# Token rows' sums on GpSimd and a newly planned order in a recurrent attention kernel on one core

## The chip, the core and the metric

The kernel runs on one core of a Trainium2 chip. A core has a matrix engine (TensorE, PE in the profile, with its weight loads shown apart as PEld), VectorE (DVE), ScalarE (ACT), GpSimd (POOL) and SyncE (SP, which issues most DMAs). The engines run their own instruction streams in order and wait for each other by semaphores. The metric is device time of one launch in microseconds; lower is better.

## What is computed

A block of a language model: attention with a recurrent memory, then an MLP, both behind a layer norm and both added to the residual. The attention walks over 64 segments of 32 tokens, and each segment's 8 memory rows come from the segment before it. That is what makes the 64 steps sequential.

```python
x = A_x                                            # (1, 2048, 512)
h  = x + A(layernorm(x), mem0, Wq, Wk, Wv, Wo)     # 32 heads of 128
h2 = h + gelu(layernorm(h) @ w1 + b1) @ w2 + b2    # 512 -> 1792 -> 512

def A(x, mem, ...):
    for s in range(64):
        hs = concat([mem, x[32*s : 32*s + 32]])    # 8 memory rows + 32 tokens
        q, k, v = hs @ Wq, hs @ Wk, hs @ Wv
        p = softmax(where(mask, q @ k.T * scale, -1e9))
        o = (p @ v) @ Wo
        mem = o[:8]                                # into the next segment
        outs.append(o[8:])
```

The mask lets every row see the memory rows and makes the rest causal.

## The kernel before

**Tiling.** A segment's left operand is `hT`, 32 columns per chunk of 128 inputs: 24 token rows (`NA`) and the 8 memory rows. The matrix engine is used in four column groups of 32, so one "unit" of a projection is four matmuls of 128 x 32 weights (the tokens) against 512 columns of WQ, WK or WV. A half of a projection (`Q0`, `Q1`, `K0`, `K1`, `V0`, `V1`) has four units, one per chunk of the 512 inputs. The other 8 tokens of each segment are handled four segments at a time: block `bk` of 128 tokens has its 4 x 8 such rows in `hB`, and their projections and output projection are the filler parts `F0` and `F1`, run one block ahead (and one behind for the output, `wo_B`) in segments of blocks 1 to 14.

**One segment.** The parts are: projections; `SC0`, `SC1`, the scores of the memory and late rows, by `ZC` and `KALL`; their softmax on DVE and ACT (`nmc` row maximum, `Ea` and `EC` the exponentials of two halves, `ra`, `rsc` reciprocals, `PCa`, `PC` the normalised rows, `PTC` their transpose); `PV0`, `PV1` (times V), whose memory rows are copied to `OT` as `OTm0`, `OTm1`; `WO`, the output projection, in eight units; `SA`, the scores of the 24 token rows, whose softmax (`nma`, `SAs`, `SAe`, `sma`, `rsa`, `PA`, `PTA`, `BD`) feeds `PVA` in the *next* segment, copied to `OT` as `OTx`. So token rows run one segment behind for PV and two behind for WO, and only memory rows are in the recurrence.

**The end of a segment.** `wo` (L1179) leaves the projection in a PSUM bank as two halves, on partitions 0 to 63 and 64 to 127. DVE transposes it to `TT` (L1183) and adds the halves, by `halves_add` (L1176), twice each: for the memory rows into `hT` of the next segment (`hTm`, L1186), and for the token rows into `opT` (`opA`, L1195). When a block's `opT` is complete, `nat` transposes it by DMA and adds it to the residual.

**The order.** `ORDERS` (L37) gives the order of the units on the matrix engine, one list for each of s mod 4, written out by hand. All other operations are placed by a list scheduler that runs when the kernel is built (`schedule`, L236): each operation has an assumed duration; `PLAN` (L43) gives many of them a due time within the segment, by s mod 4; those without (`planned`, L108, returns None) are ranked by their distance to the end. Ready operations are taken by this key and put on their engine at the first gap that fits. Some may run on either of two or three engines; the scheduler picks the cheaper or the one named in `HOME` (L100). `BANK` (L42) gives each part its PSUM bank. `PHASE` (L25) fixes at which instruction of a segment the engine's blocks of 256 instructions begin, by adding weight loads. `directions` (L580) decides in which direction a part walks over the chunks so that loaded weights can be kept between parts. POOL's folds of the block rows (`fold`, L1232, called by `tail`, L1437) wait for PC of the second half and for the `opA` adds moved into the tail.

Of the kernel before, what the change touches and what calls it, by code (L numbers as in the profile page):

```python
# [24 lines left out]
PHASE = (0, 64, 128, 192)  # L25
# [11 lines left out]
ORDERS = ((('Q0', 0, 1), ('K0', 0, 1), ('Q0', 1, 2), ('K0', 1, 2), ('Q0', 2, 3), ('Q1', 0, 1), ('Q0', 3, 4), ('K0', 2, 4), ('Q1', 1, 4), ('K1', 0, 4), ('SC0', 0, 99), ('V0', 0, 1), ('V1', 0, 1), ('V0', 1, 4), ('F1', 0, 1), ('SC1', 0, 99), ('V1', 1, 2), ('F1', 1, 2), ('V1', 2, 4), ('F0', 0, 1), ('PV0', 0, 99), ('PVA', 0, 99), ('F1', 2, 3), ('WO', 0, 2), ('PV1', 0, 99), ('WO', 2, 8), ('F1', 3, 4), ('SA', 0, 99), ('F0', 1, 4)),  # L37
# [3 lines left out]
ORDER = ORDERS[0]  # L41
BANK = dict(K0=7, K1=6, Q0=6, Q1=5, V0=7, V1=5, F0=4, F1=6, FB=4, SA=5, WO=7, SC0=3, SC1=2)  # L42
PLAN = {"kq2": (1.72,) * 4,  # L43
        "QT0": (2.37,) * 4,
        "ZCm0": (2.85,) * 4,
        "kq0": (2.23,) * 4,
        "KA0": (2.87,) * 4,
        "SP0": (-1.81, -1.81, -1.52, -1.65),
        "nmc0": (3.86,) * 4,
        "Ea0": (4.18,) * 4,  # L50
        "EC0": (4.59,) * 4,
# [1638 lines left out]
```

## Time and profile before

| | us |
|---|---|
| median of 3 runs (807.34 to 808.39) | 807.91 |
| span of the profiled execution | 805.9 |
| PE / DVE / ACT / POOL busy | 775.0 / 621.0 / 527.1 / 349.6 |
| before the first segment's end, 0 to 51.64 | 51.64 |
| segments 1 to 63 (51.64 to 702.65) | 651.01 |
| MLP and the last outputs (702.65 to 805.90) | 103.25 |

The profile is one execution; its span is 2.0 us under the median of the runs. In a row of the timeline the columns are the start, the length, the engine, the line of the kernel, the operation, out<-in by the program's names and how many were merged. A row of the table of stretches has the length, and each engine's busy time and instructions, the granted clock and the DMA share.

### The profile page before, as it was taken

What the parts mean: (1) busy time and instruction counts of PE and PEld (TensorE: products, weight loads), DVE (VectorE), ACT (ScalarE), POOL (GpSimd) and SP (SyncE); (2) the same over time, 40 slices, a digit from 0 to 9 for tenths busy, and PEclk for the clock granted to TensorE, in tenths of its full rate; (3) what the DMA queues carried; (4) which work ended last, traced back from release to release, by engine and by line L of the source; (5) the groups of instructions that cost most, each with busy time, mean ns of one, the idle gap of its engine ahead of it and who ended that gap; (6) DMA issues with size and microseconds to landing.
All of it is one profiled execution on the core that took longest, in us unless ns stands there. A gap on an engine that the chain in (4) does not pass through costs nothing.

```text
span 805.9 us, 43594 instructions
## 1 busy us (share of the span) xinstructions
PE 775.0 (96%) x19308; PEld 422.5 (52%) x18891; DVE 621.0 (77%) x2008; ACT 527.1 (65%) x1522; POOL 349.6 (43%) x886
## 2 busy tenths in 40 slices
PE   3788999999999999999999999999999999999998
PEld 1345555555555555555555555555555555544443
DVE  3268897989898989898989898989899887824211
ACT  2446777777777777777777777777676766643342
POOL 5023334545454545454545454545463535267200
PEclk9989999999999999999999999999999999999999
DMA  9950010111101010101010202020212131264200
GB/s 340 392 185 16 4 29 11 30 31 29 31 21 39 17 43 17 43 11 50 9 45 10 50 11 50 11 49 3 51 29 62 40 86 29 88 170 130 69 27 26
DMA packets 65449, 48.03 MB, mean 60 GB/s; under 512 B 29028, under 2 KB 61676, under 8 KB 65260
## 3 DMA queue, kind: packets, MB, share of 16 engines
q1 hardware_dynamic: 64928, 44.98, 19.0%
q8 instruction: 150, 2.46, 1.2%
q14 instruction: 39, 0.32, 0.1%
q10 hardware_dynamic: 332, 0.27, 0.1%
HBM read 31.08 MB, written 8.13 MB: 49 GB/s over the span
## 4 chain that ended last, share of the span: by engine, by line
PE 91%; DVE 3%; DMA 2%; SPq 2%; ACT 1%; issue 1%; POOL 0%
PE ps L872 43%; PE ps L1171 16%; PE ps L605 6%; PE quad L1579 6%; PE ps L1572 5%; PE ps L1210 4%; PE quad L1075 3%; DMA WQ<-in_A_Wq_dram 2%; SPq L775 2%; PE ps L1105 2%; PE quad L1037 2%; PE ps L1365 2%; PE quad L1143 1%; PE quad L1080 1%; DVE PC L1062 1%; ACT kq L890 1%
## 5 line engine op out<-in xcount | busy, mean ns | idle before, releaser
L872 PE MATMUL ps<-WQ,hT 128*32 128x512 bf16 x2048 | 157.4, 382 | 3.4 <-DVE hT L1177 3.3
L1171 PE MATMUL ps<-WO,OT 128*32 128x256 bf16 x4224 | 140.8, 275 | 1.0 <-ACT OT L890 1.0
L872 PE MATMUL ps<-WV,hT 128*32 128x512 bf16 x1780 | 138.7, 379 | 0.0
L891 ACT ACTIVATE kq<-ps 128x512 bf16<-128x512 f32 x146 | 87.2, 597 | 63.7 <-PE ps L872 63.4
L1126 POOL TENSOR_TENSOR PA<-SA,rsa 128x256 bf16<-128x256 f32 x64 | 39.9, 624 | 183.0 <-DVE rsa L1119 170.6
L890 ACT CAST kq<-ps 128x512 bf16<-128x512 f32 x160 | 93.4, 584 | 38.2 <-PE ps L872 38.2
L1171 PEld LDWEIGHTS ps<-WO,OT 128*32 128x32 bf16 x4224 | 96.2, 97 | 26.5 <-ACT OT L890 12.3
L1132 POOL COPY BD<-PTA 32x192 bf16<-32x192 bf16 x256 | 95.5, 373 | 16.6 <-DVE PTA L1128 0.8
L1062 DVE SCALAR_TENSOR_TENSOR PC<-EC,rsc,even 128x128 bf16<-128x128 f32 x256 | 94.5, 370 | 6.7
L872 PE MATMUL ps<-WK,hT 128*32 128x512 bf16 x1292 | 92.5, 379 | 0.0
L872 PEld LDWEIGHTS ps<-WQ,hT 128*32 128x32 bf16 x2048 | 57.0, 96 | 57.9 <-issue 18.7
L913 DVE STREAM_TRANSPOSE KALL<-kq 128x256 f32<-128x256 f32 x160 | 70.5, 440 | 20.8 <-ACT kq L890 18.6
L1054 ACT ACTIVATE EC<-quad,nmc 128x64 f32<-128x64 f32 x252 | 77.1, 311 | 5.9 <-DVE nmc L1045 0.2
L605 PE MATMUL ps<-WK,hT 128*32 128x512 bf16 x756 | 74.6, 379 | 0.0
L890 ACT CAST VS<-ps 128x512 bf16<-128x512 f32 x126 | 73.7, 585 | 0.7
L890 ACT CAST OT<-quad 128x128 bf16<-128x128 f32 (+1 forms) x205 | 66.3, 363 | 7.5 <-PE quad L1080 5.7
L913 DVE STREAM_TRANSPOSE QT<-kq 128x256 f32<-128x256 f32 x128 | 57.0, 445 | 15.5 <-ACT kq L891 14.1
L872 PEld LDWEIGHTS ps<-WV,hT 128*32 128x32 bf16 x1780 | 50.5, 96 | 34.2 <-issue 1.0
L1575 ACT ACTIVATE WQ<-ps,b1t 128x512 bf16<-128x512 f32 x42 | 28.9, 688 | 52.0 <-PE ps L1572 52.0
L872 PEld LDWEIGHTS ps<-WK,hT 128*32 128x32 bf16 x1292 | 36.4, 97 | 46.1 <-issue 20.1
L1117 ACT ACTIVATE SA<-SA 128x256 f32<-128x256 f32 x64 | 26.7, 417 | 49.4 <-DVE SA L1116 45.0
L1223 POOL TENSOR_TENSOR opT<-TTB,TTS 32x64 bf16<-32x64 f32 x128 | 40.3, 315 | 31.7 <-DVE opT L1177 22.5
(160 smaller groups left out, 1477.9 us busy)
## 6 DMA issues: line engine op xcount, KB each, us to landing
WV<-in_A_Wv_dram SPq DMA_DIRECT2D x4, 1024.0 KB, 10.3
WK<-in_A_Wk_dram SPq DMA_DIRECT2D x4, 1024.0 KB, 18.0
WQ<-in_A_Wq_dram SPq DMA_DIRECT2D x4, 1024.0 KB, 19.0
WO<-in_A_Wo_dram SPq DMA_DIRECT2D x16, 256.0 KB, 7.6
v_last<-VSB SPq DMA_DIRECT2D x60, 64.0 KB, 3.1
VBD<-v_last SPq DMA_DIRECT2D x60, 64.0 KB, 2.8
h_mid<-xr SPq DMA_DIRECT2D x16, 128.0 KB, 1.8
WQ<-h_mid SPq DMA_DIRECT2D x4, 512.0 KB, 4.4
```

The lines of the kernel that those rows point to most:

```text
L605: return e.add_instruction(mybir.InstMatmult(name="I-%d" % (4000000 + _kept[0]), engine=mybir.EngineType.PE, start_tensor_calc=start, stop ...
L872: ins = e.matmul(o, l, m, start=(k == 0), stop=(k == DC - 1), tile_position=(0, 32 * j), skip_group_check=True)
L890: return {"act": (lambda e: e.copy(out, src), t_act(n, ps_)), "dve": (lambda e: e.tensor_copy(out, src), 0.155 + 1.0e-3 * n * fast)}
L891: return {"act": (lambda e: e.mul(out, src, scale_), t_act(n, ps_)), "dve": (lambda e: e.tensor_scalar(out, src, scale_, None, ALU.mult), ...
L913: S.op("dve", lambda e: e.transpose(out, src), reads=[("kq", i)], writes=[key], dur=t_dve(256) + 0.02)
L1054: return e.activation(EC[:, r, sl, :], o[:, sl, :], ACTF.Exp, bias=nmc[:, r, sl:sl + 1], accum_out=smc[:, r, sl:sl + 1])
L1062: S.op("dve", lambda e, sl=sl, xc=xc: e.scalar_tensor_tensor(PC[:, r, :, :, sl], xc, rsc[:, r, sl:sl + 1], ev, ALU.mult, ALU.mult), reads= ...
L1132: S.narrow(S.op("pool", lambda e, j=j, rows=rows: e.tensor_copy(BD[rows, par, :, j, :, :], PTA[rows, :, 0:NA, :]), reads=["PTA"], writes=[ ...
L1171: ins = e.matmul(ps[bank][32 * j:32 * j + 32, 0:256], lhs(slot(h)), wo_cols(h, b), start=(k == 0), stop=(k == 15), tile_position=(0, 32 * ...
L1223: return e.tensor_tensor(o[32 * q:32 * q + 32, c:c + 2], x, y, ALU.add)
L1572: ins = e.matmul(ps[bank][:, 0:SBT], W1[:, cc, fc * P:(fc + 1) * P], hnT_of(k)[:, cc, :], start=(cc == 0), stop=(cc == DC - 1))
L1579: S.op("pe", lambda e: e.matmul(quad[:, t, :], gT_of(k, fc)[:, t * P:(t + 1) * P], W2[:, fc, :], start=(fc == 0), stop=(fc == FC - 1)), re ...
```

## The change

- `wo`: the sum of the token rows' halves (`opA`) moves from DVE to POOL: one copy of partitions 0 to 63 of `TT` (token columns, `opS`) to partitions 64 to 127 of the scratch tile `TTS`, now 128 partitions high, then two adds, each on 64 partitions.
- `schedule`: operations without a due time get their rank scaled to the segments' pace and 2.1 us of lead; a planned operation may not be put ahead of one that was planned earlier on the same engine.
- `ORDERS`: K0 goes first in a segment, Q0 is done after six or seven units, SA goes behind the filler units in segments 0, 1 and 2 mod 4. `directions` is worked out for each of the four orders.
- `PLAN` and `HOME` are new throughout, each due time by s mod 4; `BANK` moves Q0 from bank 6 to bank 0; `PHASE` moves by 21 places.
- Eight banks become one PSUM tensor, `PC` and `PTC` become two tiles each, `b1n` lies in `oN`. The diff also has branches (`TT2`, `SPL`, `KCOL`, `PVM`, `NRM`, `P3`) whose switches are off.

```diff
-PHASE = (0, 64, 128, 192)
+PHASE = (235, 43, 107, 171)
+OPA = True
+AHEAD = 2.1
-ORDERS = ((('Q0', 0, 1), ('K0', 0, 1), ('Q0', 1, 2), ('K0', 1, 2), ('Q0', 2, 3), ('Q1', 0, 1), ('Q0', 3, 4), ('K0', 2, 4), ('Q1', 1, 4), ('K1', 0, 4), ('SC0', 0, 99), ('V0', 0, 1), ('V1', 0, 1), ('V0', 1, 4), ('F1', 0, 1), ('SC1', 0, 99), ('V1', 1, 2), ('F1', 1, 2), ('V1', 2, 4), ('F0', 0, 1), ('PV0', 0, 99), ('PVA', 0, 99), ('F1', 2, 3), ('WO', 0, 2), ('PV1', 0, 99), ('WO', 2, 8), ('F1', 3, 4), ('SA', 0, 99), ('F0', 1, 4)),
...
+ORDERS = ((('K0', 0, 1), ('Q0', 0, 2), ('K0', 1, 2), ('Q0', 2, 4), ('Q1', 0, 1), ('K0', 2, 4), ('Q1', 1, 4), ('K1', 0, 4), ('SC0', 0, 99), ('V0', 0, 4), ('V1', 0, 1), ('F1', 0, 1), ('SC1', 0, 99), ('V1', 1, 3), ('F1', 1, 2), ('F0', 0, 1), ('V1', 3, 4), ('PV0', 0, 99), ('PVA', 0, 99), ('F1', 2, 3), ('WO', 0, 2), ('PV1', 0, 99), ('WO', 2, 8), ('F1', 3, 4), ('F0', 1, 4), ('SA', 0, 99)),
...
-BANK = dict(K0=7, K1=6, Q0=6, Q1=5, V0=7, V1=5, F0=4, F1=6, FB=4, SA=5, WO=7, SC0=3, SC1=2)
+BANK = dict(K0=7, K1=6, KX=3, Q0=0, Q1=5, V0=7, V1=5, F0=4, F1=6, FB=4, SA=5, WO=7, SC0=3, SC1=2, SC2=1, PV0=7)
...
-        "VS1": (6.72,) * 4,
-        "OTm0": (6.56,) * 4,
-        "nma": (10.17,) * 4,
-        "PTA": (13.52,) * 4,
-        "BD": (15.41,) * 4,
-        "TT": (9.37,) * 4,
-        "hTm": (9.86,) * 4,
-        "opA": (17.5, 10.96, 18.73, 17.5),
+        "BD": (16.331, 0.007, 16.734, 15.95),
+        "OTm0": (5.545, 5.337, 3.85, -0.582),
+        "PTA": (13.188, 14.525, 13.433, 12.556),
+        "TT": (6.905, 7.221, 7.098, 0.097),
+        "VS1": (6.687, 6.87, 6.634, 6.858),
+        "hTm": (3.099, 7.229, 6.437, 5.811),
+        "nma": (-6.06, -1.636, 0.66, 3.743),
+        "opA0": (8.087, 8.613, 0.69, 8.76),
+        "opA1": (-1.074, 4.255, -1.419, -0.739),
+        "opS": (17.639, 3.506, 18.616, 20.489),
...
-HOME = {('SC0', 0): 'act', 'ZCm0': 'pool', 'kq1': 'act', 'SP1': 'act', 'VS1': 'act', 'OTm0': 'act', 'SAp': 'dve', 'PA': 'pool', 'VSB1': 'act'}
+HOME = {'SP1': 'act', 'SAp': 'dve', 'ZCm1': 'pool', 'ZCm0': 'pool', 'OTx0': 'dve', ('SA', 2): 'act', ('SC0', 0): 'dve', 'kq3': 'act', ('SC0', 3): 'dve', 'kq0': 'act', 'OTm1': 'act', ('SA', 1): 'act', 'kq4': 'act', ('SA', 0): 'act', ('SC1', 1): 'dve', 'VSB1': 'act'}
...
+        first, pace = base[1], 4 * STEP / (base[6] - base[10])
...
-                key = -o.rank - BONUS.get(o.kind, 0.0)
+                key = -(first - (first - o.rank) * pace) - AHEAD - BONUS.get(o.kind, 0.0)
...
-                i = bisect.bisect_right(ST, t)
+                i = max(bisect.bisect_right(ST, t), placed[eng] + 1 if fixed else 0)
...
+            if fixed:
+                placed[o.eng] = i
+            elif i <= placed[o.eng]:
+                placed[o.eng] += 1
...
-        TTS = sb("TTS", [64, 2, 4, 32], F32)
+        TTSX = sb("TTS", [P, 2, 4, 32], F32)
+        TTS = TTSX[0:64]
...
-                    o_ = S.op("dve", lambda e: [halves_add(tt, q2, o[64 * q2:64 * q2 + 64], slice(0, NA))(e) for q2 in range(2)][1],
-                         reads=[("TT", par)], writes=[("opA", (sx // 4) % 2, sx % 4)], dur=0.53, after=after)
+                    if OPA:
+                        v = TTSX[64:128].rearrange("p c q t -> p (c q t)")[:, 0:2 * DC * NA].rearrange("p (c q t) -> p c q t", c=DC, q=2)
+                        S.narrow(S.op("pool", lambda e: e.tensor_copy(v, tt[0:64, :, :, 0:NA]), reads=[("TTl", par)] * TT2 + [("TT", par)], writes=["opS"], dur=0.35, after=after))
+                        for q2 in range(2):
+                            S.narrow(S.op("pool", lambda e, q2=q2: e.tensor_tensor(o[64 * q2:64 * q2 + 64], tt[64:128, :, q2, 0:NA], v[:, :, q2], ALU.add),
+                                          reads=["opS", ("TT", par)] + [("TTl", par)] * TT2, writes=[("opA%d" % q2, (sx // 4) % 2, sx % 4)], dur=0.4, after=after))
+                        S.tag = was
+                        return
...
-                elif s % 4 in (3, 0) and 3 < s < NS - 2:
+                elif s % 4 in (3, 0) and 3 < s < NS - 2 and not OPA:
                     now.append(rows)
```

More of the change, by code (lines that the diff above doesn't have):

```diff
@@ L295, in schedule @@
         starts = {e: [] for e in ENGINES}
+        placed = {e: -1 for e in ENGINES}
         for o in order:
@@ L1027, in sc_mm @@
             reg = 2 + bk % 2
+            heads = range(4) if part is None else range(2 * part, 2 * part + 2)
             def f(e):
-                for i in range(4):
+                for i in heads:
                     for j in range(4):
@@ new lines, in normal, with pv_spread @@
+            S.op("dve", lambda e: e.transpose(PTC[r][:].rearrange("p k t a -> p (k t a)").bitcast(F32), PC[r][:].rearrange("p k t a -> p (k t a)").bitcast(F32)),
+                 reads=[("PCa", r)] * (not NRM >> r & 1) + [("PC", r)], writes=[("PTC", r)], dur=0.31)
+        def pv_spread(s):
+            for j in range(4):
+                rows = slice(32 * j, 32 * j + 32)
+                o, v = PB[rows, j].rearrange("p t a -> p (t a)"), PTC[0][rows, 0].rearrange("p t a -> p (t a)")
+                x = S.either({"act": (lambda e, o=o, v=v: e.copy(o, v), 0.26), "dve": (lambda e, o=o, v=v: e.tensor_copy(o, v), 0.2), "pool": (lambda e, o=o, v=v: e.tensor_copy(o, v), 0.3)},
+                             reads=[("PTC", 0)], writes=[("PB", j)])
+                x.thin = True
@@ L1081, in f @@
+                    ins = e.matmul(o, VBD[rows, bk % 2, sg, r, :], PTC[r][rows, :, 32:64, :].rearrange("p b q a -> p b a q"),
                                    start=False, stop=True, tile_position=(64 * t, 0), skip_group_check=True)
                 return ins
[L1083 to L1084 removed]
+            S.op("pe", f, reads=[("VS", s % 3, r), ("PTC", r)] + [("VBD", bk % 2, j) for j in range(4)], writes=both, dur=0.205, mode=MH, ni=20)
```

397 lines of the change are left out of this document (271 added, 126 removed), and 6 rows, old and new, of the table ORDERS.

## The prediction

> **What bounds the kernel now.** I read the page's busy shares first, then the busy time by stretches, each of four segments, that is one block of 128 tokens.
>
> ```profile
> span 805.9 us, 43594 instructions
> PE 775.0 (96%) x19308; PEld 422.5 (52%) x18891; DVE 621.0 (77%) x2008; ACT 527.1 (65%) x1522; POOL 349.6 (43%) x886
> core 0: us, PE busy (x) PEld busy (x) DVE busy (x) ACT busy (x) POOL busy (x), PEclk, DMA share, GB/s
> 244.77:285.92 41.15, 41.15 (x1172) 23.04 (x1125) 37.09 (x123) 30.07 (x91) 20.14 (x53) 1.00 0.12 29
> 285.92:327.07 41.15, 41.15 (x1172) 22.96 (x1125) 37.09 (x123) 30.07 (x91) 20.26 (x53) 1.00 0.11 29
> 615.54:657.34 41.80, 41.54 (x1173) 23.04 (x1125) 37.28 (x125) 30.28 (x91) 19.52 (x50) 1.00 0.19 51
> ```
>
> Four segments take 41.15 us again and again, 10.29 each, with PE covered from end to end. But PE rows overlap and their ends are modelled, so short waits hide in them. They come out by subtracting starts. The timeline of PE through one segment:
>
> ```profile
> 270.39 0.40 PE L605 MATMUL ps<-WK,hT 128*32 128x512 bf16 x4
> 270.61 0.83 PE L872 MATMUL ps<-WK,hT 128*32 128x512 bf16 x12
> ...
> 273.65 0.40 PE L872 MATMUL ps<-WV,hB 128*32 128x512 bf16 x4
> 274.00 0.26 PE L1075 MATMUL quad<-PTC,VS 64*128 64x32 bf16 x8
> 274.11 0.22 PE L1080 MATMUL quad<-PTC,VBD 64*128 64x128 bf16 x2
> ...
> 274.46 0.40 PE L872 MATMUL ps<-WV,hB 128*32 128x512 bf16 x4
> 274.75 0.62 PE L1171 MATMUL ps<-WO,OT 128*32 128x256 bf16 x16
> 275.31 0.26 PE L1075 MATMUL quad<-PTC,VS 64*128 64x32 bf16 x8
> 275.42 0.22 PE L1080 MATMUL quad<-PTC,VBD 64*128 64x128 bf16 x2
> 275.57 1.50 PE L1171 MATMUL ps<-WO,OT 128*32 128x256 bf16 x48
> 276.89 0.42 PE L1105 MATMUL ps<-KALL,QT 128*32 128x32 bf16 x32
> 277.14 1.06 PE L872 MATMUL ps<-WV,hB 128*32 128x512 bf16 x16
> 278.07 0.41 PE L872 MATMUL ps<-WQ,hT 128*32 128x512 bf16 x4
> ```
>
> A unit of four 512-wide matmuls costs 0.22 (270.39 to 270.61). Three places cost more. The unit at 273.65 takes 0.35 until PV0: 0.13 over. The unit at 274.46 takes 0.29 until WO: 0.07 over. The four units at 277.14 take 0.93 where 0.86 would do: 0.07 over. WO's 16 matmuls at 274.75 take 0.56 until PV1, where 16/48 of 1.32 (275.57 to 276.89) would be 0.44: 0.12 over. The 0.12 before PV1 is the nearest row for what a change of tile shape costs on PE, so of PV0's 0.13 only about 0.01 is a wait. The other two are waits, as the table of waits shows:
>
> ```profile
> PEld L870 <- DVE hT L1177: 24.8, 62, 1.3
> PEld ps L1171 <- ACT OT L890: 12.3, 62, 0.3
> PEld quad L1075 <- DVE rsc L1059: 31.6, 64, 0.9
> ```
>
> Each occurs in nearly every segment. The weight loads run ahead, so those sums are larger than what PE loses. So about 0.15 us of the 10.29 can be won by order, some 1.5%; the rest is matmuls and shape changes, which the diff leaves alone in number and kind.
>
> **What the change does, part by part.**
>
> *The wait before WO.* WO waits for OTm0, ACT's copy of PV0's memory rows. On ACT:
>
> ```profile
> 273.95 0.58 ACT L890 CAST VS<-ps 128x512 bf16<-128x512 f32 x1
> 274.42 0.29 ACT L890 CAST OT<-quad 128x128 bf16<-128x128 f32 x1
> ...
> 275.68 0.27 ACT L890 CAST OT<-quad 128x128 bf16<-128x128 f32 x1 [0.18 <-PE quad L1080]
> ```
>
> Here the second cast (PV1's copy) starts 0.26 after its last matmuls (275.42 to 275.68), on an ACT that was idle. The first starts 0.31 after (274.11 to 274.42): it stands behind the VS1 cast. In the new plan OTm0 has key 5.5, 5.3, 3.9, -0.6 and VS1 6.7, 6.9, 6.6, 6.9, and a planned operation may no longer be put ahead of an earlier planned one on its engine; so OTm0 goes first and VS1 follows. That saves 0.31 - 0.26 = 0.05. It is realised in full, since WO can move 0.07 before the unit ahead of it bounds it. VS1 then ends about 274.37 + 0.29 + 0.58 = 275.24, and PV1 starts at 275.31: just hidden. If that cover is gone, VS1's lateness takes back up to the 0.05. A unit stands between PVA and WO in blocks 1 to 14, 56 segments: 56 x 0.05 = **-2.8 us**.
>
> *The sums of token rows leave DVE.* Rows of what goes and of the nearest to what comes:
>
> ```profile
> L1177 DVE TENSOR_TENSOR opT<-TT 64x96 bf16<-64x96 f32 x128 | 33.8, 264 | 3.0
> L1225 POOL COPY TTS<-TTB 64x256 f32<-64x256 f32 x32 | 12.6, 393 | 36.2 <-DVE opT L1177 34.4 <-DVE TTB L1214 0.9
> L1226 POOL TENSOR_TENSOR TTB<-TTB,TTS 64x256 f32<-64x256 f32 x32 | 23.1, 722 | 14.2 <-DVE PC L1062 12.6
> L1223 POOL TENSOR_TENSOR opT<-TTB,TTS 32x64 bf16<-32x64 f32 x128 | 40.3, 315 | 31.7 <-DVE opT L1177 22.5
> ```
>
> Two adds per segment, 0.53 us, leave DVE, 33.8 us in all. POOL gets a copy of 192 columns (at most 0.39, as for 256) and two adds of 96 columns: 722 - 315 over 192 columns is 2.1 ns each, so 315 + 32 x 2.1 = 382 ns. Together 0.39 + 0.76 = 1.15 us a segment, 74 us in all. POOL has 41.15 - 20.14 = 21.0 us free in four segments, so 4.6 of it is covered. DVE's relief is worth nothing directly: the three DVE chains in PE's way run back to back from what ACT and PE release, and the opT adds were in none of them. What it does free is POOL's folding of TTB, which waited for those adds (the 34.4 and 22.5 above). How a fold collides with the adds of hTm, the last link before the next segment:
>
> ```profile
> 267.29 0.43 DVE L1177 TENSOR_TENSOR hT<-TT 64x32 bf16<-64x32 f32 x2
> 277.61 0.39 DVE L1177 TENSOR_TENSOR hT<-TT 64x32 bf16<-64x32 f32 x2
> 586.38 0.51 DVE L1177 TENSOR_TENSOR hT<-TT 64x32 bf16<-64x32 f32 x2
> 267.08 0.39 POOL L1225 COPY TTS<-TTB 64x256 f32<-64x256 f32 x1
> 586.32 1.14 POOL L1223 TENSOR_TENSOR opT<-TTB,TTS 32x64 bf16<-32x64 f32 x3
> ```
>
> 0.39 beside no such fold, 0.43 beside POOL's copy, 0.51 beside its adds. In segments 1 mod 4 (267.29) the fold came late because it waited for opT; now it can be earlier: -0.04 x 14 = -0.6. Against it the new copy may start right after the transpose to TT (key 3.5 in those segments), at the same place: +0.04 x 14 = +0.6. I take **0**, and 0.12 x 56 = 6.7 us as the upper bound, if every hTm meets an add; the lower bound is -0.6.
>
> The Trainium skill, "SBUF — State Buffer", section "Who interferes with whom", says that a VectorE instruction with two SBUF inputs and a GpSimd one that reads SBUF take one port pair as an exclusive lock, and that the second blocks until the first is done. By that rule a collision would cost hTm up to a whole POOL add, 0.37, and the bound would be 21 us. The rows show 0.12, so I keep that.
>
> *The order on PE.* K0 comes first, Q0 is complete after six or seven units in place of seven, K0 after eight or nine in place of nine; SC0 stays after 16, SC1 and PV0 behind the same count of units. SA moves behind the filler units F. Between WO's end and the next segment stand four units and SA as before, so the wait for hTm stays at 0.07: **0**. SA's product, though, ends 0.93 later. Its chain:
>
> ```profile
> 278.03 0.42 DVE L1115 TENSOR_REDUCE nma<-ps 128x8 f32<-128x256 f32 x1
> ...
> 282.39 1.68 POOL L1132 COPY BD<-PTA 32x192 bf16<-32x192 bf16 x4
> ...
> 284.41 0.30 PEld L1143 LDWEIGHTS quad<-BD,VS 64*128 64x128 bf16 x16
> ```
>
> nma stood behind hTm, 0.89 after SA's end on PE (277.14 to 278.03), so SA's end moves to 278.07, and nma, released some 0.2 after it as ACT's second cast was (0.26 after the start of the last matmuls), to about 278.25: 0.22 later. BD ends at 284.07, 0.34 before PVA wants it; 0.12 is left: 0. The other bound is that PTA, BD and the copies on POOL queue behind the new adds by 0.1 more than that; 0.1 x 56 = +5.6 us.
>
> *Unplanned operations at one pace, fetch phase.* What isn't planned, layer norms, loads and folds, is ranked by a scaled rank. It can move the stretches outside the steady pace: the block 615.54 shows 41.80, 0.65 over 41.15, and the block before and after it are over too. I take 0; from below -1.5 (two such blocks and a half cured), from above the same. The instruction blocks of PE now begin 21 places later in a segment. One row shows what a bad place costs:
>
> ```profile
> 338.80 0.57 PE L1105 MATMUL ps<-KALL,QT 128*32 128x32 bf16 x32
> 339.19 0.83 PE L872 MATMUL ps<-WK,hB 128*32 128x512 bf16 x12
> ```
>
> SA takes 0.39 there (338.80 to 339.19) in place of 0.25 (276.89 to 277.14), with an instruction transfer nearby. Bounds: 0.14 in every segment would be 9 us, none 0; nearest is the common segment, which shows none: 0.
>
> **Sum.** 805.9 - 2.8 = 803.1 for the profiled execution. The median of the runs is 807.9, 2.0 over the span; the same 2.0 gives **805.1**.
>
> **Rivals.** (1) *More is cured*: the new keys also shorten the chain to PV0 or hTm, so half of the remaining 0.10 goes: 56 x 0.05 more, to 802.3, range 799 to 803. For it: all three waits are dependencies. Against: the keys from SC0 to PTC0 keep nmc0, KA1, the reciprocals, nmc1, PC0 in their sequence. (2) *OTm0 isn't moved*, or VS1 takes the gain back at PV1: 807.9. For it: the slack of 0.07 before PV1. (3) *Slower: POOL's adds beside hTm.* The new copy is released by the very transpose that releases hTm's adds. If copy and adds of the segment before and this one stand there in every segment, each hTm costs 0.12 more: +6.7 - 2.8 = +3.9, 811.8. It decides from 2.8/0.12 = 23 segments with a collision on. Against: keys of 17.6 and more in three segments of four put the copy behind BD, in the stretch that POOL has free. By the lock of the skill's page the same collisions would give 807.9 + 0.37 x 56 - 2.8 = 826; a row for it is missing.
>
> **Chances and range.** The forecast 0.50 (803.5 to 806.2), more cured 0.14, nothing net 0.17, slower 0.19 (809.6 to 814). A measurement of this kernel tells about 0.2%, 1.6 us, from no change. Faster 0.64, same 0.17, slower 0.19. Leaving out about one in ten on either side gives 801 to 811.5; the forecast's own range is 803.5 to 806.2.
>
> **What would show it.** Right: four steady segments take 40.95; OT's first cast starts 0.26 after PV0's last matmuls, ahead of the VS cast; 0.02 over in place of 0.07 before WO; POOL near 424 us busy, DVE near 587; no opT row on DVE. Wrong: hT's pair at 0.5 beside POOL's new rows, PVA waiting for BD, PV1 waiting for VS, SA rows of 0.39 everywhere, or 41.15 as before.

## The result, and the profile after

Forecast 805.1 us (801.0 to 811.5, faster 0.64). Measured: **827.5 us** (825.45 to 828.09, 4 runs) against 807.75 (807.34 to 808.39) for the kernel before on the same chip; ratio 1.0238, 95% interval 1.0221 to 1.0255. The change makes the kernel 19.75 us slower: outside the range, and on the other side.

The page of the changed kernel, first its busy shares, then two groups of POOL (busy, mean ns, idle before):

```profile
span 825.6 us, 43682 instructions
PE 781.5 (95%) x19308; PEld 422.2 (51%) x18817; DVE 611.4 (74%) x1950; ACT 509.8 (62%) x1452; POOL 420.5 (51%) x1078
L1350 POOL TENSOR_TENSOR opT<-TT,TTS 64x96 bf16<-64x96 f32 x128 | 52.1, 407 | 10.2
L1348 POOL COPY TTS<-TT 64x192 f32<-64x192 f32 x64 | 22.9, 358 | 11.5 <-DVE TT L1333 8.2
```

On POOL the work moved as costed: it is busy 420.5 (424 forecast), with as many matmuls as before. VectorE is not: 611.4 where 587 was forecast. The new `HOME` sends `OTx0` there, and its casts of 128x384 go from 50 to 110 on DVE (25.1 to 56.5 us busy) and from 78 to 18 on ACT, which nearly fills what the sums left free. The span is 19.7 us longer for the same matmuls, so the loss lies in waits, and for a small part in a lower clock at the beginning. The busy time by stretches says where. The three stretches are the beginning up to segment 4, segments 4 to 59 (those with filler), and the rest; before, then after:

```profile
0.00:82.61 82.61, 57.10 (x1269) 30.31 (x1393) 42.51 (x127) 37.39 (x104) 24.34 (x82) 0.94 0.64 228
82.61:659.79 577.18, 576.87 (x16353) 323.85 (x15710) 516.70 (x1716) 421.08 (x1274) 274.42 (x704) 1.00 0.12 31
659.79:805.90 146.11, 140.98 (x1692) 68.30 (x1806) 61.84 (x167) 68.64 (x144) 50.88 (x100) 1.00 0.28 78
```

```profile
0.00:86.99 86.99, 58.90 (x1268) 29.95 (x1360) 41.38 (x121) 37.09 (x104) 25.61 (x85) 0.92 0.61 216
86.99:675.75 588.76, 580.96 (x16352) 323.67 (x15668) 510.85 (x1675) 404.96 (x1205) 336.38 (x872) 1.00 0.12 30
675.75:825.60 149.85, 141.63 (x1692) 68.61 (x1805) 59.16 (x156) 67.75 (x143) 58.56 (x121) 1.00 0.29 77
```

Head +4.38, middle +11.58, tail +3.74: 19.70 us in all. The prediction's sum has terms for the middle alone.

**The middle, from segment to segment.** Lengths from the first projection matmul of one segment to that of the next, medians of the 13 segments of each kind, s = 4 to 55:

| s mod 4 | 0 | 1 | 2 | 3 | four |
|---|---|---|---|---|---|
| before | 10.281 | 10.331 | 10.275 | 10.269 | 41.16 |
| after | 10.466 | 10.486 | 10.278 | 10.445 | 41.67 |

Kind 2 is as fast as before; the others lose 0.155 to 0.185. The timeline of the changed kernel in a segment of kind 1, from PC1 to PV1's weight load (start, length, engine, line, operation), and then the next segment, of kind 2:

```profile
313.76 0.74 DVE L1159 SCALAR_TENSOR_TENSOR PC<-EC,rsc,even 128x128 bf16<-128x128 f32 x2
...
313.86 0.94 POOL L1350 TENSOR_TENSOR opT<-TT,TTS 64x96 bf16<-64x96 f32 x2
313.96 0.27 ACT L950 CAST OT<-banks 128x128 bf16<-128x128 f32 x1 [0.32 <-PE banks L1221]
...
314.13 0.59 ACT L950 CAST VS<-banks 128x512 bf16<-128x512 f32 x1
...
314.28 0.62 PE L1319 MATMUL banks<-WO,OT 128*32 128x256 bf16 x16
314.54 0.31 DVE L1161 STREAM_TRANSPOSE PTC<-PC 128x128 f32<-128x128 f32 x1
...
314.97 0.20 PEld L1216 LDWEIGHTS banks<-PTC,VS 64*128 64x128 bf16 x8 [0.34 <-ACT VS L950]
...
324.24 0.62 DVE L1159 SCALAR_TENSOR_TENSOR PC<-EC,rsc,even 128x128 bf16<-128x128 f32 x2
...
324.61 0.59 ACT L950 CAST VS<-banks 128x512 bf16<-128x512 f32 x1
...
324.89 0.31 DVE L1161 STREAM_TRANSPOSE PTC<-PC 128x128 f32<-128x128 f32 x1
...
325.32 0.19 PEld L1216 LDWEIGHTS banks<-PTC,VS 64*128 64x128 bf16 x8 [0.22 <-ACT VS L950]
```

OTm0 goes first now, 0.26 after PV0's last matmuls (313.70 on PE, line L1221), as forecast, and VS1 stands behind it. The profile names VS as PV1's releaser both times. The ends say otherwise. In kind 1, VS ends at 314.13 + 0.59 = 314.72, 0.25 before the load; PTC ends at 314.54 + 0.31 = 314.85, 0.12 before it. In kind 2 both end at 325.20, 0.12 before the load. Only PTC's distance is the same in both: **PTC1 releases PV1**. Over s = 4 to 55 the median from PTC1's end to PV1's first matmul is 0.147 in all four kinds (0.146 in kind 2); from VS1's end it is 0.15 to 0.29. PTC1 is late in kind 1 because PC's two operations take 0.74 in place of 0.62, and beside them run POOL's two adds of the token rows. The medians of that stretch are 0.70, 0.75, 0.62 and 0.75 in the four kinds, with one, two, no and two of these adds beside it. (In the kernel before, the stretch is 0.83, with a reciprocal between the two operations, but it begins at 6.23 of the segment in place of 6.41.)

**Single stalls.** Five segments of kind 3 (s = 7, 27, 35, 39, 59) are 1.0 to 1.2 longer still, each in the middle of WO. The rows at one of them:

```profile
419.32 0.50 PE L1319 MATMUL banks<-WO,OT 128*32 128x256 bf16 x12
...
420.75 0.29 PE L1319 MATMUL banks<-WO,OT 128*32 128x256 bf16 x4 [0.93 <-issue]
```

No engine that the profile shows is waited for. But the trace has the transfers of instructions (queue q8, 150 of them). In the five segments with a stall, such a transfer begins at 5.97 to 6.06 of the segment, and WO goes on 1.42 to 1.56 after it has landed; the longest transfer (1.16, the others 0.88 to 0.98) stands before the longest stall (1.16, the others 0.93 to 0.97). In the nine other segments of kind 3 from 7 to 59, it begins at 2.1 to 4.7. That marks the stalls as waits for code. In kind 0 the lengths also scatter, from 10.33 to 10.70. In the waits of PE the five add up to the first row here:

```profile
PE banks L1319 <- issue: 4.9, 5, 1.2
PE banks L1291 <- ACT EC L1127: 2.9, 3, 1.0
PE banks L1107 <- POOL ZC L996: 1.8, 1, 1.8
```

**Head and tail.** Segment 0 is 1.21 longer than before (26.08 against 24.87). The rows of nearly all of it, before and after, have the granted clock third from the end:

```profile
36.62:51.64 15.02, 12.12 (x212) 5.96 (x221) 6.57 (x24) 5.75 (x19) 0.75 (x3) 0.66 1.00 314
36.62:52.85 16.23, 13.01 (x211) 6.22 (x220) 6.56 (x24) 5.75 (x19) 0.74 (x2) 0.61 0.98 301
```

TensorE was granted half the clock for 10.24 us of segment 0 before, for 13.65 us after. In all 18 traces of this case the segment's length goes with that time: 24.3 to 24.6 us with 6.83 us at half clock, 24.7 to 25.5 with 10.24, 26.0 to 26.2 with 13.65. Changed kernels stand in each of the three groups, and in the last also experiment 4, which has the old plan. So these 1.2 us are not a cost that the new order is shown to have.

The other two rows of waits lie in segments without filler. Segment 1 is 2.95 longer than before; its timeline:

```profile
58.42 0.75 POOL L1280 COPY BD<-PTA 32x192 bf16<-32x192 bf16 x2
...
59.23 0.29 POOL L996 COPY ZC<-QT 128x128 bf16<-128x128 bf16 x1
...
59.57 0.31 PE L1107 MATMUL banks<-KALL,ZC 128*32 128x64 bf16 x16 [1.76 <-POOL ZC L996]
...
61.28 0.27 ACT L950 CAST OT<-banks 128x128 bf16<-128x128 f32 x1 [2.34 <-PE banks L1221]
61.45 0.32 ACT L1127 ACTIVATE EC<-banks,nmc 128x64 f32<-128x64 f32 x1
...
62.21 0.37 PE L1291 MATMUL banks<-BD,VS 64*128 64x48 bf16 x16 [0.97 <-ACT EC L1127]
```

ZCm1, on the way of the recurrence, stands on POOL behind BD, which nobody needs yet; and the exponentials of the second half stand on ACT behind OTm0, which waits 2.34 for PV0. With filler on PE both come in time; without it they are what PE waits for. Segments 60, 61 and 62 show the second of the two (+1.24, +0.97, +0.45, together 2.66 of the tail's 3.74).

### The profile page after: what moved, and what is told of

Its sections match the earlier page's. It is cut to its first block, busy times and chain, and to the rows that moved or that the text cites. A ratio compares the mean times of both kernels' runs of the same rounds, so it can differ in the third digit from the quotient of the medians.

```text
span 825.6 us, 43682 instructions
## 1 busy us (share of the span) xinstructions
PE 781.5 (95%) x19308; PEld 422.2 (51%) x18817; DVE 611.4 (74%) x1950; ACT 509.8 (62%) x1452; POOL 420.5 (51%) x1078
## 4 chain that ended last, share of the span: by engine, by line
PE 85%; DVE 3%; DMA 3%; POOL 3%; SPq 2%; issue 2%; ACT 2%; POOLq 0%
PE banks L913 39%; PE banks L1319 15%; PE banks L638 9%; PE banks L1761 4%; PE banks L1754 4%; PE banks L1216 4%; PE banks L1369 3%; DMA WQ<-in_A_Wq_dram 2%; SPq L813 2%; PE banks L1107 2%; PE banks L1253 2%; PE banks L1291 1%; PE banks L1221 1%; DVE PC L1159 1%; POOL opT L1382 1%
## 5 line engine op out<-in xcount | busy, mean ns | idle before, releaser
L1319 PE MATMUL banks<-WO,OT 128*32 128x256 bf16 x4224 | 141.6, 275 | 5.4 <-issue 4.9
L913 PE MATMUL banks<-WV,hT 128*32 128x512 bf16 x1780 | 132.3, 379 | 0.0
L913 PE MATMUL banks<-WQ,hT 128*32 128x512 bf16 x1480 | 121.1, 382 | 0.0
L913 PE MATMUL banks<-WK,hT 128*32 128x512 bf16 x1416 | 117.0, 381 | 3.4 <-DVE hT L1325 3.3
L951 ACT ACTIVATE kq<-banks 128x512 bf16<-128x512 f32 x146 | 87.4, 599 | 40.8 <-PE banks L913 36.6
L950 ACT CAST kq<-banks 128x512 bf16<-128x512 f32 x160 | 93.7, 585 | 29.4 <-PE banks L913 26.1
L1319 PEld LDWEIGHTS banks<-WO,OT 128*32 128x32 bf16 x4224 | 97.4, 97 | 27.1 <-issue 7.6
L1127 ACT ACTIVATE EC<-banks,nmc 128x64 f32<-128x64 f32 x256 | 78.3, 311 | 15.1 <-DVE nmc L1118 15.0
L950 ACT CAST VS<-banks 128x512 bf16<-128x512 f32 x126 | 74.0, 588 | 0.0
L638 PE MATMUL banks<-WK,hT 128*32 128x512 bf16 x632 | 65.5, 379 | 0.1
L950 DVE CAST OT<-banks 128x384 bf16<-128x384 f32 x110 | 56.5, 524 | 1.8 <-PE banks L1291 1.8
```

What stands on the lines that cost most here:

```text
L638: return e.add_instruction(mybir.InstMatmult(name="I-%d" % (4000000 + _kept[0]), engine=mybir.EngineType.PE, start_tensor_calc=start, stop ...
L913: ins = e.matmul(o, l, m, start=(k == 0), stop=(k == DC - 1), tile_position=(0, 32 * j), skip_group_check=True)
L950: return {"act": (lambda e: e.copy(out, src), t_act(n, ps_)), "dve": (lambda e: e.tensor_copy(out, src), 0.155 + 1.0e-3 * n * fast)}
L951: return {"act": (lambda e: e.mul(out, src, scale_), t_act(n, ps_)), "dve": (lambda e: e.tensor_scalar(out, src, scale_, None, ALU.mult), ...
L1127: return e.activation(EC[:, r, sl, :], o[:, sl, :], ACTF.Exp, bias=nmc[:, r, sl:sl + 1], accum_out=smc[:, r, sl:sl + 1])
L1319: ins = e.matmul(ps[bank][32 * j:32 * j + 32, 0:256], lhs(slot(h)), wo_cols(h, b), start=(k == 0), stop=(k == 15), tile_position=(0, 32 * ...
```

## The experiments

Times are medians against the kernel before on the same chip. The kernel before measured 807.7 to 808.7 in these groups.

**1. Code phases.** The changed kernel with the old `PHASE`.

```diff
-PHASE = (235, 43, 107, 171)
+PHASE = (0, 64, 128, 192)
```

> The changed kernel with the old PHASE (0, 64, 128, 192). Theory F (the blocks of instructions now begin at places where PE has no slack): the five stalls of about 1.0 us in front of WO's last unit in segments 3 mod 4 and some 0.2 us in each segment 0 mod 4 go, together 8 us: about 819.5. Rival theory O (the new order of operations on ACT, DVE and POOL makes the time, and the fetch stalls are a consequence of its slips): within 2 of 827.5, with stalls of the same size in other places.

820.82 us, ratio 1.0160 (1.0145 to 1.0176). The stalls are gone, kind 0 has a median of 10.335 in place of 10.466, and the middle is 5.90 shorter:

```profile
87.02:669.88 582.86, 578.54 (x16353) 319.09 (x15669) 510.15 (x1675) 404.98 (x1205) 335.52 (x872) 1.00 0.12 31
```

**2. VS1 first, by its due time.** A miss.

```diff
-"OTm0": (5.545, 5.337, 3.85, -0.582), "VS1": (6.687, 6.87, 6.634, 6.858)
+"OTm0": (6.56, 6.56, 6.56, 6.56), "VS1": (5.0, 5.0, 5.0, 5.0)
```

> The changed kernel with the due times of VS1 (5.0) and OTm0 (6.56) set so that ACT casts VS1 before OTm0, as in the kernel before. Theory V (PV1 now waits for VS1): the 0.25 to 0.38 us from WO's second unit to PV1 go back to 0.22, WO's wait for OTm0 returns to 0.29, net -0.05 x 56 = -3 us; in segments 1, 60 and 61, where OTm0 stood before the exponentials of the second half, another 3 to 4 us: about 821. Theory F: within 2 of 827.5 or the five stalls of 1.0 elsewhere.

870.77 us, ratio 1.0776 (1.0760 to 1.0792). Due at 5.0, VS1 came ahead of the second half's exponentials, and by the new rule these can no longer be put ahead of it. PVA waits for them 31 times:

```profile
PE banks L1291 <- ACT EC L1127: 36.1, 31, 1.4
```

It says nothing on VS1; it shows that under the rule a due time is an order.

**3. The sum back on DVE**, in the new plan.

```diff
-OPA = True
+OPA = False
```

> The changed kernel with the token rows' sum back on DVE, all else as changed. Theory M (the move to GpSimd costs, by collisions of POOL with DVE's PC and hTm): 815 or less. Theories F, V and edge order: the move is not what costs, 824 to 829.

840.82 us, ratio 1.0412 (1.0387 to 1.0437). DVE's adds now stand ahead of hTm:

```profile
PE banks L913 <- DVE hT L1325: 16.9, 21, 3.2
```

The time is outside both expectations: the new plan is made for the sum on POOL. But here no add of POOL's lies beside PC1 in any kind; PC1's stretch is 0.61 to 0.63, and in kinds 1 to 3 PV1 starts at 7.52 to 7.53 of the segment, where the changed kernel has 7.66, 7.52 and 7.67.

**4. The move alone**, in the kernel before: copy and adds on POOL, `opS` due at 17.5 and the adds at 17.6, old plan, old order.

```diff
-S.op("dve", halves_add ..., dur=0.53)
+S.op("pool", tensor_copy(v, tt[0:64])); 2 x S.op("pool", tensor_tensor(o, tt[64:128], v, add))
-elif s % 4 in (3, 0) and 3 < s < NS - 2: now.append(rows)
```

> The kernel before with nothing changed but the token rows' sum, on GpSimd with the shifted copy, due where the DVE adds were. Theory M: slower than before by 4 to 7 us (0.12 a segment), 812 to 815. The other theories: 806 to 810, the three POOL instructions of 0.34 and 2 x 0.39 us hide in POOL's free time.

808.91 us, ratio 1.0016 (1.0006 to 1.0026): +1.1 us. Its middle is 578.24, 1.06 over. The old scheduler puts copy and adds right behind TT, so they meet hTm: its rows have a mean of 212 in place of 196 ns.

```profile
L1180 DVE TENSOR_TENSOR hT<-TT 64x32 bf16<-64x32 f32 x126 | 26.8, 212 | 3.0
```

By itself the move costs little; what more it costs in the changed kernel comes from where the new plan puts it.

**5. Old due times at the edges**, segments 0 to 3 and 60 to 63.

```diff
-return PLAN.get(k, ...)[o.tag[0] % 4]
+return (PLAN if 4 <= o.tag[0] < 60 else EDGE).get(k, ...)[o.tag[0] % 4]
```

> The changed kernel, with the old due times used for segments 0 to 3 and 60 to 63 alone. Theory (new due times, fitted to steady segments with filler, put ZCm1 behind PA and BD on POOL and OTm0 ahead of Ea1 and EC1 on ACT where there is no filler): segments 1, 60, 61 and 62 lose their extra 2.95, 1.24, 0.97 and 0.45 us, so 827.5 - 5.6 = 821.9 us, and no wait of PVA for EC1 of about 1 us is left. Rival (those segments are slow because of code loading or the different order on TensorE): no change, 827 to 828.

823.74 us, ratio 1.0207 (1.0190 to 1.0224). Head 84.32 and tail 146.37: 2.67 and 3.48 shorter, of which 1.0 lies in segment 0, with 10.24 us at half clock. Segment 1 keeps 1.45 of its loss, again behind POOL's ZC.

**6. VS1 directly ahead of OTm0**, behind EC1 this time.

```diff
-"OTm0": (5.545, 5.337, 3.85, -0.582), "VS1": (6.687, 6.87, 6.634, 6.858), "SAp": (6.127, 0.763, 8.735, 3.543)
+"OTm0": (6.12,) * 4, "VS1": (6.1,) * 4, "SAp": (7.5, 7.5, 8.735, 7.5)
```

> The changed kernel with VS1 put after EC1 and directly ahead of OTm0 on ScalarE (in the changed kernel it stands directly behind OTm0), SAp behind both. Theory: VS1's 0.27 us behind OTm0 is what PV1 waits for in steady segments; the wait of PV1 for VS1 (16.2 us in the changed kernel's waits) goes, the gap between WO's first 16 matmuls and PV1 falls from about 0.33 to 0.215 us, WO's own wait rises from 0.23 to 0.29: net 56 x (0.115 - 0.06) = -3 us, 824.4 us. Rival (VS1's lateness is covered by something else that is late too): only WO's wait changes, +3.4 us, 831.

823.06 us, ratio 1.0192 (1.0174 to 1.0209), but not for the theory's reason: the segments are as long as in the changed kernel (10.460, 10.498, 10.301, 10.475). PVA's waits for EC1 in the tail are gone, which makes the tail 3.4 shorter; two stalls for issue were left of five, 1.2 us of waits in place of 4.9, and the middle is 1.0 shorter. Kind 1:

```profile
314.15 0.58 ACT L950 CAST VS<-banks 128x512 bf16<-128x512 f32 x1
...
314.63 0.27 ACT L950 CAST OT<-banks 128x128 bf16<-128x128 f32 x1
314.95 0.34 PEld L1319 LDWEIGHTS banks<-WO,OT 128*32 128x32 bf16 x16 [0.27 <-ACT OT L950]
```

VS1 can start only when V1 is done, and the new order puts V1's last unit directly ahead of PV0 in kinds 0, 1 and 3: its last matmul ends at 6.26 to 6.28 of the segment, where before it was 6.04. So VS1 delays OTm0 and WO, and PV1 starts as late as in the changed kernel. Kind 2, with V1 done at 6.05 and no add beside PC1, is a clean comparison: 10.301 against 10.278. **OTm0 ahead of VS1 is worth 0.02 a segment**, not 0.05.

**7. The edits of experiments 1, 5 and 6 together** (`PHASE`, `EDGE`, `OTm0`, `VS1` and `SAp` as there).

> The changed kernel with the old phases of code loading, VS1 ahead of OTm0, and the old due times in segments 0 to 3 and 60 to 63: three suspected causes undone at once. Theory (they are separate and add up): 827.5 - 6.7 - 3.0 - 5.6 = 812.2 us; the remaining 4 us are PC's slower adds beside POOL and the order on TensorE at the segment's start. Rival (they overlap, one loss hides another): 816 or more. Second rival (they are all): 808.

818.33 us, ratio 1.0136 (1.0117 to 1.0155). The gains do not add up. Experiment 6 had most of its own from the tail, the same 3.4 us that 5 wins back there; and the steady segments are as long as in 6 (41.73 for four, in experiment 1 41.52).

**8. Without the rule** that keeps planned operations in order of due time.

```diff
-i = max(bisect.bisect_right(ST, t), placed[eng] + 1 if fixed else 0)
+i = max(bisect.bisect_right(ST, t), placed[eng] + 1 if False else 0)
```

> The changed kernel without the new rule that a planned operation may not be put ahead of another planned one on its engine (the old rule for placing, with the new due times). Theory (the due times are good, the rule makes an order that holds ready work back): ACT and POOL fill their gaps again, segments 1 and 60 to 62 recover, 827.5 - 5 = 822 or less. Rival (the new due times were fitted with the rule and fall apart without it): slower than 828, with DVE's or ACT's operations standing before those on the chain.

816.25 us (ratio 1.0100, 1.0080 to 1.0120, without one of the four runs, which took 4326 us). Head and tail are those of the kernel before:

```profile
0.00:82.51 82.51, 57.43 (x1268) 29.58 (x1361) 42.42 (x126) 37.20 (x103) 25.79 (x87) 0.96 0.65 228
...
668.78:814.50 145.72, 140.82 (x1692) 69.68 (x1805) 58.09 (x157) 67.60 (x140) 58.19 (x120) 1.00 0.28 79
```

Head and tail together are 8.6 shorter than in the changed kernel, of 11.1 for the whole span; 1.6 of it lies ahead of segment 1, with 6.83 us at half clock. So the rule, with due times that suit the steady segments, is the whole loss of segments 1 to 3 and the tail. There was no stall of about 1 us for issue, under the new phases. The steady segments are no better (41.79 for four).

What holds them is another operation that the rule had kept in its place. From PV1's first matmul to WO's last it is 1.63 in kinds 0, 1 and 3, where the changed kernel and experiment 16 have 1.485; the same in experiments 11, 14 and 15. Kind 1 in experiment 15:

```profile
350.70 0.23 PE L1221 MATMUL banks<-PTC,VBD 64*128 64x128 bf16 x2
...
350.93 0.27 ACT L1081 COPY banks<-maskCF 128x128 f32<-128x128 f32 x1
351.13 0.26 ACT L950 CAST OT<-banks 128x128 bf16<-128x128 f32 x1
...
351.44 0.55 PEld L1319 LDWEIGHTS banks<-WO,OT 128*32 128x32 bf16 x22 [0.24 <-ACT OT L950]
```

A copy of a mask stands on ACT ahead of OTm1, PV1's cast, which starts 0.41 after PV1's last matmuls in place of 0.25, and WO waits for it. So the rule costs about 7 us in head and tail, and spares 0.15 in three steady segments of four.

**9. The sum's copy right behind TT**, in all kinds.

```diff
-"opS": (17.639, 3.506, 18.616, 20.489)
+"opS": (3.506, 3.506, 3.506, 3.506)
```

> The changed kernel with one due time other: opS (POOL's copy for the sum) 3.506 in all four kinds of segment instead of 17.6, 3.5, 18.6 and 20.5, which puts copy and adds of segments 0 and 1 of a block right behind TT, at the start of the next segment; of segment 2 only the copy comes early, its adds still run after BD in segment 3. Theory (POOL's adds beside PC1's two operations on VectorE make PC1 0.13 us longer; PTC1 comes 0.13 later and PV1 waits for it, though the profile names VS): in segments 0 and 1 no POOL add overlaps PC1, its stretch is 0.62 instead of 0.70 and 0.75, PV1 starts at 7.52 to 7.55 of the segment instead of 7.66 and 7.68; segment 3 stays at 7.67. 28 x 0.13 = -3.6 us, less up to 0.05 in each where the adds now lie beside hTm (+1.4): about 824.5 us. Rival (PV1 waits for VS1, which stands behind OTm0): PV1 stays at 7.66 and 7.68, time 827.5 or a little above.

825.85 us, ratio 1.0214 (1.0196 to 1.0233). Kind 1 of that kernel:

```profile
313.03 0.62 DVE L1159 SCALAR_TENSOR_TENSOR PC<-EC,rsc,even 128x128 bf16<-128x128 f32 x2
...
313.40 0.59 ACT L950 CAST VS<-banks 128x512 bf16<-128x512 f32 x1
...
313.68 0.31 DVE L1161 STREAM_TRANSPOSE PTC<-PC 128x128 f32<-128x128 f32 x1
...
314.13 0.17 PEld L1216 LDWEIGHTS banks<-PTC,VS 64*128 64x128 bf16 x8 [0.21 <-ACT VS L950]
```

PC1 is back at 0.62. PV1 starts at 7.53 in kind 1 (7.66 in the changed kernel), and 0.58 after WO in kind 0 (0.67), with VS1 untouched behind OTm0; in kind 3, whose adds stay beside PC1, at 7.68 (7.67). Kinds 0 and 1 are 10.351 and 10.353 long, 0.115 and 0.133 shorter; kind 3 is 0.06 longer, since hTm there meets the adds now and ends 0.927 after TT's start in place of 0.874. The theory of VS1 falls; that of PC1 holds. Five stalls for issue are still there, in other segments (4.8 us).

**10. Sum behind TT, old phases, old edges**: the edits of 9, 1 and 5.

> The changed kernel with opS due at 3.506, the old phases of code loading and the old due times in segments 0 to 3 and 60 to 63; OTm0 stays ahead of VS1. Theory (separate losses add up): 827.5 - 2.5 - 6.7 - 3.7 = 814.6 us; what is left are segment 1 (ZCm1 behind BD, +1.5), segment 3 (adds beside PC1, 14 x 0.15) and the beginning. Rival (losses hide one another): 818 or more.

817.36 us, ratio 1.0109 (1.0086 to 1.0133), between theory and rival; kinds 0 to 2 at 10.249, 10.358, 10.274, kind 3 at 10.475.

**11. Sum behind TT and no rule**: the edits of 9 and 8.

> The changed kernel with opS due at 3.506 and without the rule that keeps planned operations in the order of their due times. Theory: e8_free_order's 816.3 us, in which POOL's adds lay beside PC1 in one kind of segment only; if they still do there, the same within 1 us; if they leave it, 14 x 0.13 = -1.8, 814.5. Rival (e8's gain was luck of the code loading, which one moved operation upsets): 820 or more with waits for issue of about 1 us on TensorE.

816.33 us, ratio 1.0094 (1.0074 to 1.0114): no stalls, but also no better than experiment 8.

**12. The kernel before with the new phases.**

```diff
-PHASE = (0, 64, 128, 192)
+PHASE = (235, 43, 107, 171)
```

> The kernel before with the new phases of code loading (235, 43, 107, 171) alone. Theory A (the new phases by themselves let the code's transfers meet other DMA traffic): some stalls for issue of about 1 us in the middle of WO, as in the changed kernel, +3 to +7 us, 811 to 815. Theory B (which instructions lie where a fetch lands is set by phases and order together; the stall is a matter of the pair): within 1 us of 807.9, without such stalls.

808.58 us, ratio 1.0007 (0.9996 to 1.0018); its middle is 577.19. The new phases alone cost nothing. The stalls belong to the pair of phases and order.

**13. Copy and adds behind PTC1.** The kernel before held its adds in segments 3 and 0 behind PTC1; the change drops that condition. Here it is back, and the adds held for segment 3 go there too.

```diff
-elif s % 4 in (3, 0) and 3 < s < NS - 2 and not OPA:
+elif s % 4 in (3, 0) and 3 < s < NS - 2:
     now.append(rows)
...
 while held:
-    held.pop()()
+    late.append(held.pop())
```

> The changed kernel with the sum's copy and adds kept behind PTC1 in the segments 3 and 0 of a block (as the kernel before did with its adds on VectorE, a condition that the change drops), and the adds held for segment 3 behind its PTC1 too. Theory (POOL's adds beside PC1 are the whole of PV1's lateness): no POOL add of the sum lies beside PC1 in any kind of segment, PV1 starts at 7.52 to 7.55 in all four, and hTm has no add beside it that it had not before: 42 segments x 0.135 = -5.7 us, 821.8. Rival (in segment 3, where moving opS alone did nothing, something else is late): segments 0 and 1 recover only, 824.

828.94 us, ratio 1.0250 (1.0229 to 1.0271). As a time a miss. PC1 takes 0.61 in all kinds, and PV1 starts at 7.52 in kinds 1 and 2, at 7.57 in kind 3 (7.67 before this edit; a stall lies ahead of it in four segments of this kind). But kind 0 reaches PC1 0.05 later than in the changed kernel, four stalls for issue remain (3.6 us), and the tail is 1.6 longer, with 3.41 us at half clock in it that the changed kernel's tail doesn't have:

```profile
673.66:825.10 151.44, 143.37 (x1692) 69.15 (x1805) 59.24 (x156) 67.67 (x143) 58.60 (x121) 0.99 0.29 76
```

**14 and 15. The same without the rule**: the edits of 13 and 8, with the new phases, and with the old ones.

> The same, and without the rule that keeps planned operations in the order of their due times; new phases. Theory: head and tail as in e8_free_order (82.5 and 145.7 us), the middle 586.3 less 14 x 0.14 for segment 3 (the only kind that had an add beside PC1 there): 814.3 us. Rival: the free order finds other places for the adds and segments 0 and 1 stay 0.1 to 0.2 over: 816.

> As e14_sum_behind_PTC1_free with the old phases of code loading. Theory: the free order had no stalls for issue under the new phases, so the phases change nothing: the same as e14 within 1.5 us. Rival: stalls come back here, because the old phases fit the old order only: 3 us or more above it.

816.08 (ratio 1.0094, 1.0074 to 1.0114) and 814.08 us (1.0072, 1.0054 to 1.0089). Kind 3, with no add beside PC1, goes from 10.617 in experiment 8 to 10.433 and 10.410. Kinds 0 and 1 stay at 10.40 to 10.52, as the rival of 14 says, largely for the mask copy shown at experiment 8. Between the two phases lie 2.0 us, more than the theory of 15 allows and less than its rival asks; stalls of 1 us there are none.

**16. Sum behind PTC1, old phases, old edges**: the edits of 13, 1 and 5.

> The changed kernel with the sum behind PTC1, the old phases of code loading, and the old due times in segments 0 to 3 and 60 to 63; the rule, the new order on TensorE, OTm0 ahead of VS1 and the sum on POOL stay. Theory (the three losses are separate and are nearly all of it): head 84.3, middle 577.5 to 579, tail 146.3, plus 2 outside the span: 810.8 us, of which 1.5 are segment 1 behind BD. Rival (something else in the new plan still costs 3 us or more in the middle): 814 or more.

814.99 us, ratio 1.0078 (1.0055 to 1.0102). PV1 starts at 7.49, 7.53, 7.52 and 7.51 in the four kinds, and kind 3 is 10.289 long, where experiment 10, with its adds still beside PC1, had 10.475: kind 3 has the same cause as the other two. The steady segments are nearly those of the kernel before (41.29 for four; the rest is hTm in kind 0, 0.99 after TT's start in place of 0.87). Yet the rival holds:

```profile
84.60:666.24 581.64, 579.06 (x16352) 320.64 (x15668) 507.31 (x1676) 405.01 (x1204) 333.62 (x871) 1.00 0.12 31
```

14 blocks of 41.29 would be 578.1; 3.5 us more are in the middle, most of it in single longer segments, s = 49, 53 to 55 and 58, by 0.15 to 1.3 each. The longest, 55, on DVE:

```profile
623.13 0.41 DVE L1565 TENSOR_SCALAR xn<-xT,agg,rst 128x512 bf16<-128x512 bf16 x1 [1.91 <-DMA xT<-h_mid]
623.46 0.44 DVE L1390 STREAM_TRANSPOSE TT<-banks 128x256 f32<-128x256 f32 x1
```

A layer norm of the MLP, begun early to save time at the end, stands ahead of TT and waits 1.91 us for its load; the recurrence waits with it. In experiments 1 and 10 the same segment is 11.29 and 11.62 long, in the changed kernel 10.55. That is a matter of unplanned operations and of when the load lands. In 49 and 53 one of PC0's operations takes 0.55, beside POOL's copies to BD, and PV0 comes 0.19 later. In 54 and 58 the first half's ZC stands on POOL behind PA and the adds ahead of it, at 3.24 and 3.41 of the segment in place of 2.82 in segment 50, and SC0 waits. The tail has one stall for issue left, 0.82 in segment 63.

None of these kernels beats the kernel before.

## Why the prediction was wrong

| | us | shown by |
|---|---|---|
| segments 1 to 3 and the tail, by the rule and due times made for steady segments | +6.9 | 8 (whole), 5 (5.2 of it) |
| stalls and other waits that the old phases take away | +5.9 | 1, 12 |
| POOL's adds beside PC1, 14 x (0.086 + 0.130 + 0.135) | +4.9 | 9; 1 against 10 and 16 |
| segment 0, longer at half clock in the profiled execution | +1.2 | its rows |
| sum | 18.9 of 19.7 | |

The first three are nearly the loss, but undone together (experiment 16) they gave back 12.5 us of it: segment 1 stays 1.5 over, behind the rule, and each edit made some other segments longer. So the sum of single gains is not a proof that nothing else costs.

*The wait before WO.* The move was as forecast: OTm0 ahead of VS1, its cast 0.26 after PV0's matmuls, and in kind 2 WO starts at 6.95 of the segment, where experiment 6, with VS1 first, has 7.00. The failed step is "It is realised in full" with its cover, "VS1 then ends about 274.37 + 0.29 + 0.58 = 275.24, and PV1 starts at 275.31: just hidden." PV1 had to move 0.05 ahead as well, and it has two inputs, VS1 and PTC1. PTC1, which the prediction didn't look at, already ended only 0.11 before PV1, and the profile before named it as PV1's releaser:

```profile
274.89 0.31 DVE L1064 STREAM_TRANSPOSE PTC<-PC 128x128 f32<-128x128 f32 x1
...
275.30 0.17 PEld L1075 LDWEIGHTS quad<-PTC,VS 64*128 64x128 bf16 x8 [0.21 <-DVE PTC L1064]
```

Nor were the 0.07 for VS1 shown to be a cover: in kind 2 of the changed kernel both inputs end together, 0.12 before the load and 0.15 before PV1. There, with nothing else in the way, PV1 starts at 7.52 (7.55 in experiment 6), and 0.02 of the 0.05 was left. Against the kernel before even that is gone: PV0 starts at 6.24 in place of 6.21 there.

*The sums leave DVE.* The number of operations, their durations and POOL's time were right, and PVA doesn't wait for BD, as reckoned; DVE's time was not, since `HOME` was left out. The mechanism of rival 3, POOL's adds beside a VectorE operation with two SBUF inputs, was right too, and the price near: 0.12 from the rows, 0.09 to 0.135 measured, though for another operation, so that is partly luck. hTm itself did not pay it: its rows have a mean of 197 ns in place of 196. So it is chance as well that rival 3's 826, by the lock, lies near the 827.5 measured. The failed step is the place. The prediction looked at hTm alone and took "the stretch that POOL has free" behind BD as safe; in that stretch DVE runs PC1, on the recurrence. Free time of the engine that gets the work was asked for, and not what the other engine does then.

The Trainium skill, "SBUF — State Buffer", section "Who interferes with whom", names this collision, and the traces agree that it happens. They do not show that the second operation blocks until the first is done. The two operations of PC and the two adds beside them, in the segment of kind 1 shown above (min/median/max in ns):

```profile
L1159 DVE SCALAR_TENSOR_TENSOR PC<-EC,rsc,even x2: 343/418/493, 313.8 to 314.0; 128x128 bf16<-128x128 f32 x2
L1350 POOL TENSOR_TENSOR opT<-TT,TTS x2: 386/430/475, 313.9 to 314.4; 64x96 bf16<-64x96 f32 x2
```

The first add starts while PC's first operation has 0.24 left and takes 475 in place of 386. PC's second operation starts while that add has 0.33 left and takes 493, where kind 2, without adds, has 366 for it. So each loses 0.09 and 0.13, and not what the other had left. These are the spans that the profile gives, and it calls those on POOL rough; whether a lock is held for a part of a span can't be seen here.

*Order on PE.* Taken as 0 because the count of units ahead of each part stays. Which unit comes last was not asked: V1's, in three kinds of four, 0.22 later. With OTm0 first that costs nothing that shows (VS1 starts at 6.78 of the segment in kinds 1 and 2 alike, with V1 done at 6.25 and 6.05); experiment 6 shows that it takes the other order away.

*Unplanned pace, fetch phase.* Taken as 0 because "nearest is the common segment, which shows none". That argued from a kernel with other phases. SA rows of 0.39 were not what came, but five gaps in WO, 4.9 us in all, inside the bound of 9. The Trainium skill, "Runtime: NRT & Kernel Launch", section "Instruction fetch mechanics", calls the cost of crossing a block of code mostly hidden. Here no stall of this kind shows in the kernel before, and in the changed one 5 of the 150 transfers bring one. That it is code loading rests on two things: the old phases remove the stalls, and the late transfer of instructions is in each segment with a stall and in no other of its kind. Why the transfer begins late just there is open.

*Head and tail* had no term. The prediction read the rule as what puts OTm0 ahead of VS1, and did not ask what it holds back where a segment has no filler: ZCm1 behind BD, EC1 behind OTm0. This is the largest part, and the new plan's due times show the first: ZCm1 has 5.651 in kind 1, BD 0.007.

Still open: about 6 us that experiment 16 is over the kernel before are placed above, in segment 1, the single longer segments, kind 0 and the tail, but not undone. The new `ORDERS`, `HOME`, `BANK` and the scaled rank were not undone one by one.

## What to carry to other kernels

Work moved to an engine with free time is free only if the engine that it slows, here VectorE beside GpSimd, has nothing on the chain in that stretch: look at what runs there, not only at the links that are known to collide. A gain before one wait is a gain only if every input of the next consumer also comes earlier; compare the ends of all of them, since the releaser that a profile names may be another that ended earlier. Where an order is fixed from due times fitted to the steady state, read the first and last iterations separately: what fills the engine there is missing, and so is the cover.

## What the runs showed of the hardware

- POOL's adds and PC's two-input operation on VectorE slow each other: 0.09 on the add, 0.13 on PC, in the segment shown above. POOL's copies to BD beside PC look harmless in the median (0.377 against 0.355 in the changed kernel), but it depends on when they start: of 124 such operations of PC, 36 began within 0.045 of the start of a copy and have a median of 0.473, the others 0.359.
- Stalls for issue of about 1 us on TensorE come and go with unrelated edits: with the new phases five in the changed kernel and in experiment 9, four in 5 and 13, two in 6, none in 8 and 11; none in the kernel before with either phases. They recur at the same place of several segments of one kind, 1.4 to 1.6 after a transfer of instructions has landed.
- TensorE's clock is granted by half for 6.83, 10.24 or 13.65 us of segment 0, one time or another, and the segment takes 24.3 to 26.2 us with it. A stretch of 3.41 us at half clock lies in segment 3 of experiment 6 (12.52 us in place of 10.45), another in the tail of 13.
